# Scores of batches 3 and 4 formed transposed inside runs of small matmuls, with the runs at new steps, and loads of x released by ReLU results

## The chip, the cores and the metric

The kernel runs on one core of a Trainium2 chip. The metric is device time in microseconds (us) of one execution; smaller is better. Engines are named as in the profile: PE is TensorE (matmuls; PEld its weight loads), DVE is VectorE, ACT is ScalarE, POOL is GpSimd, and SP is SyncE, which here only issues transfers. A q behind an engine's name (SPq, POOLq) is its queue of issues.

## The reference: what is computed

There are 8 batches of 8 heads with 512 tokens each, 32 state rows per head, and 64 numbers per row; the feed-forward part has d_model 512 and d_ff 1536.

```
scores  = scale * x @ state^T            # per batch and head: 512 x 32
a       = softmax(scores)                # over the 32 state rows
xread   = a @ state                      # 512 tokens read from the state
scores2 = scale * state @ x^T            # 32 x 512
sread   = softmax(scores2) @ x           # 32 state rows read from the tokens
y       = concat([xread, sread])         # 544 rows per batch, 8 heads side by side = 512 numbers
out     = (relu(y @ w_gate) * (y @ w_val)) @ w_out
```

The output has 8 x 544 rows of 512 numbers in float32.

## The kernel before, in words

**Two products are merged.** Since `xread = a @ state`, the kernel forms `U = state @ w_gate` and `state @ w_val` once per batch (tile `U`, 256 rows of heads and states by 2 x 1536) and then `gate = a @ U`. The attention weights of a batch, transposed, are the tile `ans`.

**Step.** The main loop (line 547) runs over steps g = 12 b + jf from 28 to 107: batch b, slice jf of 128 of the 1536 columns. A step has a gate/value group (`gv`, line 319, or `gvs`, line 336, for the state rows at steps 96 to 107), four matmuls into two banks of PSUM; a ReLU of the gate on ACT (line 343, tile `g_sb`); the product with the value on DVE (line 347, tile `h_sb`); and a piece of the output product (`out_piece`, line 395), four matmuls on the `h_sb` of 18 steps ago (`lag`). Each third piece is followed by a copy on ACT (line 364) and an output transfer on SP. Then come the extra units of that step, in the order in which `at` was called for it.

**Extra units.** These prepare later batches:

- `x_load` (line 423): GpSimd issues the load of one batch of x, 512 KB after its cast to bf16, into one of four buffers `xb`.
- `x_trans_dma` (line 148): SP issues a transposing transfer from `xb` to `xT`.
- Scores, plain form (`att_sc`, line 173): eight matmuls of 64 columns for half the heads, with `xT` as weights. ACT takes the exponential to `e_sn` (line 203). A batch takes two such groups.
- Scores, transposed form (`sT_mm`, line 183): sixteen matmuls of 256 columns on 64x32 tiles of the array, eight side by side, with the state as weights, into two banks. ACT takes the exponential to `eT` (line 191), and a transposing transfer on SP turns it into `e_sn` (line 196).
- `att_norm`: for each half of the heads a sum and a reciprocal on DVE (lines 209, 211) and a scaling (line 215) on DVE or GpSimd; behind the second half, a transposing transfer on SP to `ans` (line 223).
- `u_unit` (line 292): eight matmuls of 512 columns on 64x32 tiles, a sixth of a batch's `U`; two casts out of PSUM on ACT and DVE (line 304).
- `x_pad` (line 251): two copies on GpSimd from `xb` to `xa`; `sr` (line 260): the state read `sread` of two batches, 128 matmuls of 65 columns on 128x32 tiles, normalised on DVE; `sr_T_dma` (line 274) transposes it through a transfer on SP, and `sr_out` copies it to `br` on ACT (line 278).
- `state_T_dma` (line 122) and `state_out_dma` (line 130): the state of batches 4 to 7, transposed by a transfer and copied by GpSimd.

**Runs.** `run` issues several units on small tiles one after another, because going from the whole array to small tiles and back costs time. A step with a run is in `paired`: it issues a second output piece behind the run, and the next step issues none. A run has two or three slots, a slot being a U unit or a transposed score. Before, batches 3 and 4 have plain scores, outside runs, at steps 28, 29, 39 and 40, and batches 5 to 7 transposed scores in the runs at 49, 61 and 73.

**Banks.** Eight banks of PSUM are named by tags. In the loop `bank` goes round three pairs, (4,3), (2,1), (0,5); a gate/value group takes one pair, a U unit or a transposed score too. Banks 6 and 7 hold output pieces and state reads. So in a run of three slots the third takes the pair of the gate/value group just before it, and waits for that group's ReLU and product.

**Order.** The kernel is scheduled by hand: each engine executes its instructions in the order in which the program issues them. Steps before 28 are a list of words (`program`, line 438), in which `gv.2.0@45` is the gate/value group of batch 2, slice 0, in banks 4 and 5, `re` and `mu` its ReLU and product, `dx` a load of x, `xd` a transposing transfer of x, `ad` one of attention, `xp` the pad copies. Each engine waits by semaphores for what it reads and for buffers to come free.

Of the kernel before, what the change touches and what calls it, by code (L numbers as in the profile page):

```python
# [9 lines left out]
BF16 = mybir.dt.bfloat16  # L10
# [6 lines left out]
def kernel(  # L17
# [9 lines left out]
    nc = tc.nc  # L27

    B, H, S, D = x.shape
# [34 lines left out]
    xa = const.tile([128, NX, NC * H, DP], BF16, name="xa")  # L64
# [4 lines left out]
    stT = const.tile([128, 2, B, H, Ns], BF16, name="stT")  # L69
# [2 lines left out]
    spare = hs_sb.rearrange("p f n -> p (f n)")  # L72
    warm = nc.const_aps.tensor(1.0, (128, 512), BF16)
    tiny = const.tile([128, 1], FP32, name="tiny")

    xf, xb, xT, eT, e_sn, a_sn, ANS, U, hsb = {}, {}, {}, {}, {}, {}, {}, {}, {}
    copy = {"act": nc.scalar.copy, "dve": nc.vector.tensor_copy, "pool": nc.gpsimd.tensor_copy}
# [14 lines left out]
    held = {}  # L92


    def state_dma(eng, lo, hi):
        src = state.rearrange("(g b) h (m i) d -> (b h m) g i d", b=2, i=4)
        eng.dma_start(out=st_f[:, lo // 2:hi // 2], in_=src[:, lo // 2:hi // 2])
# [64 lines left out]
    def sn_alloc(b):  # L162
        e_sn[b] = att.tile([128, 2, NC, NJ * Ns], BF16, name="e_sn", tag="e_sn", bufs=4)
        a_sn[b] = att.tile([128, 2, NC, NJ * Ns], BF16, name="a_sn", tag="a_sn")

    def att_sc(b, jp):
        if b not in e_sn:
            sn_alloc(b)
        t = held["sc", b, jp] = bank("sc_ps")
        ps = t.rearrange("p (r c j n) -> p r c j n", r=2, c=NC, j=2)  # L170
        for h in range(4 * jp, 4 * jp + 4):
            for k in range(2):
                nc.tensor.matmul(ps[:, h % 2, 2 * k:2 * k + 2, h // 2 % 2], xT[b][:, 2 * h + k], stT[:, :, b, h],  # L173
                                 start=True, stop=True)

    def sT_mm(b):

        held["sT", b] = [bank("sT_ps"), bank("sT_ps")]
        for parity in range(2):
            for j in range(NJ):  # L180
                h = 2 * j + parity
                for r in range(2):
                    nc.tensor.matmul(held["sT", b][r][32 * j:32 * j + 32, 256 * parity:256 * parity + 256],  # L183
                                     stT[64 * r:64 * r + 64, r, b, h],
                                     xT[b][64 * r:64 * r + 64, 2 * h:2 * h + 2].rearrange("p k t -> p (k t)"),
                                     start=True, stop=True)
# [232 lines left out]
    def x_load(b, part, parts):  # L419
        if part == 0:  # L420
            xb_alloc(b)
        hs = slice(H * part // parts, H * (part + 1) // parts)
        nc.gpsimd.dma_start(out=xb[b][:, hs], in_=x[b, hs].rearrange("h (p c) d -> p h c d", c=NC))  # L423
# [3 lines left out]
    def spin(n, cols=512):  # L427
        for i in range(n):
# [1 line left out]

    steps = {"spin": spin, "stc": state_conv, "stT": state_T, "sto": state_out, "xc": x_conv_pair, "xT": x_T, "on": lambda: nc.gpsimd.memset(xa[:, :, :, D:D + 1], 1.0), "dw": w_load, "dx": x_load, "ds": lambda: state_dma(nc.gpsimd, 2, B), "do": wo_dma,
             "xo": x_out, 
             "sc": att_sc, "ex": att_exp, "nr": att_sum, "nx": att_scale, "aT2": att_T2, "ao2": att_out2, "aT": att_T, "ao": att_out,
             "c": c_unit, "co": c_out, "u": u_unit, "uo": u_out, "gv": gv, "re": relu, "mu": mult, "o": out_part,
# [21 lines left out]
    gv.0.11@72 re.0.11 mu.0.11 mu.0.8 gv.1.9@63 gv.1.11@41 re.1.9 mu.1.9 gv.0.10@76 gv.1.6@20 re.1.11 re.0.10  # L458
    sc.2.1@4 gv.1.10@73 re.1.10 ex.2.1 re.1.6 mu.0.10 mu.0.9 o.0.3@6 sc.2.0@5 o.0.4 ex.2.0 o.0.0@7 mu.1.10 mu.1.11
    u.2.1.1024@43 mu.1.6 nr.2.1 uo.2.1.1024.1.act u.2.1.0@21 u.2.1.512@50 uo.2.1.512.1.act uo.2.1.1024.0.act  # L460
    uo.2.1.512.0.act uo.2.1.0.0.act nx.2.1 uo.2.1.0.1.dve o.0.1 o.0.5 stc.2.1.pool dx.3.0.1 xp.1 xp.0 xd.3 sr.1@3
    stc.3.0.pool nr.2.0 sr.0@0 nx.2.0 sn.1 u.2.0.0@14 ad.2 of.0.1.act u.2.0.1024@52 u.2.0.512@63 o.0.2 of.0.0.act
    uo.2.0.0.0.act uo.2.0.512.1.act uo.2.0.512.0.dve o.0.6@6 o.0.7 o.0.9@7 o.0.8 of.0.2.act sn.0 gv.1.8@01
    uo.2.0.0.1.dve uo.2.0.1024.0.dve gv.2.0@45 re.2.0 re.1.8 mu.1.8 gv.2.2@36 xp.3 gv.2.3@40 re.2.2 re.2.3 xp.2
    gv.2.1@31 re.2.1 mu.2.1 mu.2.3 mu.2.0 uo.2.0.1024.1.act mu.2.2
    """
    for word in program.split():
        word, _, banks = word.partition("@")
# [6 lines left out]
    units, paired = {}, set()  # L475

    def at(b, jf, f, *args):
        units.setdefault(NF * b + jf, []).append(lambda: f(*args))

    def att_up(b, kc, eng):  # L480
        att_sc(b, kc)
        att_exp(b, kc)
        att_norm(b, kc, eng)

    def att_norm(b, kc, eng):
        att_sum(b, kc)
        att_scale(b, kc, eng)
        if kc == 1:
            att_aT_dma(b)

    def run(*items):

        for it in items:
            if it[0] == "sT":
                sT_mm(it[1])
                for r in range(2):
                    sT_exp(it[1], r)
                eT_dma(it[1])
            else:
                u_unit(*it)  # L500
                for kc, eng in enumerate(("act", "dve") if len(items[0]) == 3 else ("dve", "dve")):
                    u_out(*it, kc, eng)

    def u(b, *part):
        order = (0, 0), (1, 0), (0, 512), (1, 512), (0, 1024), (1, 1024)
        return [(b, *order[i]) for i in part]

    def sr(*bs):
        sr_mm(bs, "spare")
# [2 lines left out]
    first, lag = 2 * NF + 4, 18  # L512
    for g in (2, 3):
        at(2, 2 + g, state_T_dma, g)
    for half in range(2):
        at(2, 5, state_out_dma, 2, half, "pool")
        at(2, 11, state_out_dma, 3, half, "pool")
    at(2, 5, x_load, 4, 0, 1)
    at(2, 10, x_load, 5, 0, 1)
    at(3, 10, x_load, 6, 0, 1)  # L520
    at(4, 10, x_load, 7, 0, 1)
    for b, s, jf in ((4, 2, 9), (5, 3, 6), (6, 4, 4), (7, 5, 4)):
        at(s, jf, x_trans_dma, b)
    for kc, eng in enumerate(("dve", "pool")):
        at(2, 4 + kc, att_up, 3, kc, eng)
        at(3, 3 + kc, att_up, 4, kc, "dve")
        at(4, 5 + kc, att_norm, 5, kc, "dve")
        at(5, 6 + kc, att_norm, 6, kc, "dve")
        at(6, 5 + kc, att_norm, 7, kc, "dve")
    for s, jf, items in ((2, 7, u(3, 0, 1, 2)), (2, 10, u(3, 3, 4, 5)),  # L530
                         (3, 7, u(4, 0, 1, 2)), (3, 10, u(4, 3, 4, 5)),
                         (4, 1, [("sT", 5)] + u(5, 0, 1)), (4, 10, u(5, 2, 3, 4)),
                         (5, 1, [("sT", 6)] + u(5, 5) + u(6, 0)), (5, 4, u(6, 1, 2, 3)), (5, 10, u(6, 4, 5) + u(7, 0)),
                         (6, 1, [("sT", 7)] + u(7, 1, 2)), (6, 10, u(7, 3, 4, 5))):
        at(s, jf, run, *items)
        paired.add(NF * s + jf)
    for bs, s, jf in (((2, 3), 2, 10), ((4, 5), 5, 4), ((6, 7), 6, 10)):
        at(s, jf, sr, *bs)
        at(s, jf + 1, sr_T_dma, bs)
        at(s, jf + 6, sr_out, bs, "act")  # L540
    for b, jf in ((0, 4), (1, 5)):
        at(2, jf, sr_T_dma, (b,))
        at(2, jf + 5, sr_out, (b,), "act")
    for b, s, jf in ((4, 3, 0), (5, 3, 9), (6, 5, 9), (7, 6, 0)):
        at(s, jf, x_pad, b)
    piece = first - lag
    for g in range(first, NF * (B + 1)):
        b, jf = divmod(g, NF)
# [47 lines left out]
```

## Time and profile before

| | us |
|---|---|
| median of 3 timed runs (lowest to highest) | 220.52 (220.29 to 220.78) |
| the profiled execution's own time | 219.6 |
| its span, first to last instruction | 217.8 |
| busy: PE, DVE, ACT, POOL | 213.4, 131.5, 119.3, 42.8 |
| gate/value groups, 384 matmuls (line 319) | 93.4 busy |
| output pieces, 372 matmuls (line 356) | 94.3 busy |
| plain scores, 80 matmuls (line 173) | 4.1 busy |
| transposed scores, 48 matmuls (line 183) | 1.2 busy |
| casts of U: DVE x40, ACT x32 (line 304) | 25.2, 16.7 busy |
| transfers that transpose: x, attention, scores, median to landing | 4.5, 3.1, 3.1 |

The page gives, for one execution, the busy time of each engine, the chain of work that ended last (followed back from the last instruction), and groups of instructions by line. The chain in order of time names, piece by piece, what the end of the kernel waited for. The timeline lists instructions with start and duration. "To landing" is the time from the issue of a transfer to its completion. The granted TensorE clock is full in this execution.

### The profile page before, as it was taken

Reading aid. Unit: us, or ns where it says so; the run is one execution under the profiler, and the core shown is the slowest. Engines: PE = TensorE matmul, PEld = TensorE weight load, DVE = VectorE, ACT = ScalarE, POOL = GpSimd, SP = SyncE. Lnnn points to the kernel's source line nnn. Section 1 sums busy time; section 2 is a strip of 40 time slices with the busy share of each in tenths; the row PEclk is TensorE's granted clock in tenths of the full one; section 3 lists DMA queues with packets and bytes.
Section 4 is the critical chain, followed back from the end, with each engine's and each line's share of the span. In section 5 each row is a group of like instructions: output and inputs, shape, how many; then the busy total and the mean of one; then the engine's idle time right before and its main releaser. Section 6 shows DMA issues by size and latency. Waiting matters only on the chain.

```text
span 217.8 us, 4862 instructions
## 1 busy us (share of the span) xinstructions
PE 213.4 (98%) x1957; PEld 105.2 (48%) x1957; DVE 131.5 (60%) x228; ACT 119.3 (55%) x229; POOL 42.8 (20%) x60
## 2 busy tenths in 40 slices
PE   8899999999999999999999999999999999999995
PEld 3554454454444454444444444444454445666544
DVE  5699977961986477657856778576765334222100
ACT  4698877746673666555445654764454543333222
POOL 7974049072154600000000070000000000000000
PEclk9999999999999999999999999999999999999999
DMA  7999999882879799317351651322411122222132
GB/s 166 182 195 198 199 224 164 118 207 81 120 116 156 153 201 178 89 51 158 84 101 48 132 124 21 98 62 63 102 50 60 48 48 50 51 51 85 61 96 97
DMA packets 45287, 24.44 MB, mean 112 GB/s; under 512 B 25712, under 2 KB 40944, under 8 KB 45264
## 3 DMA queue, kind: packets, MB, share of 16 engines
q0 software_dynamic: 16896, 9.05, 31.0%
q1 hardware_dynamic: 27472, 14.33, 27.6%
q10 hardware_dynamic: 896, 0.75, 1.3%
q8 instruction: 15, 0.25, 0.5%
q14 instruction: 8, 0.07, 0.1%
HBM read 18.35 MB, written 8.91 MB: 125 GB/s over the span
## 4 chain that ended last, share of the span: by engine, by line
PE 93%; DMA 3%; DVE 2%; issue 1%; POOL 0%; POOLq 0%
PE o_ps L356 40%; PE gv_ps L319 38%; PE gv_ps L336 5%; PE up L292 4%; DMA xb<-in_x_dram 3%; PE upc L292 1%; PE o_ps L385 1%; PE sr_ps L260 1%; PE xT_ps L156 1%; PE sc_ps L173 1%; DVE a_sn L215 1%; DVE cs L209 1%; PE sT_ps L183 0%; DVE xT L159 0%; DVE rc L211 0%
## 5 line engine op out<-in xcount | busy, mean ns | idle before, releaser
L356 PE MATMUL o_ps<-wo_sb,h_sb 128*128 128x512 bf16 x372 | 94.3, 379 | 0.0
L319 PE MATMUL gv_ps<-ans,U 128*128 128x512 bf16 x384 | 93.4, 379 | 0.0
L347 DVE TENSOR_TENSOR h_sb<-gv_ps,g_sb 128x512 bf16<-128x512 f32 x96 | 64.2, 687 | 46.6 <-ACT g_sb L343 45.7
L343 ACT ACTIVATE g_sb<-gv_ps 128x512 bf16<-128x512 f32 (+1 forms) x108 | 61.4, 579 | 47.2 <-PE gv_ps L319 35.0
L319 PEld LDWEIGHTS <-U 128*128 128x128 bf16 x384 | 36.8, 98 | 43.6 <-issue 0.8
L356 PEld LDWEIGHTS <-h_sb 128*128 128x128 bf16 x372 | 35.3, 98 | 41.8 <-issue 3.6
L364 ACT COPY o_sb<-o_ps 128x512 f32<-128x512 f32 x31 | 18.6, 598 | 18.6 <-PE o_ps L356 16.5
L251 POOL COPY xa<-xb 128x1024 bf16<-128x1024 bf16 x16 | 16.0, 1042 | 63.3 <-PE sr_ps L260 58.4
L304 DVE CAST U<-up 128x512 bf16<-128x512 f32 x40 | 25.2, 683 | 5.1 <-PE up L292 5.1
L304 ACT CAST U<-up 128x512 bf16<-128x512 f32 x32 | 16.7, 596 | 10.0 <-PE up L292 10.0
L347 DVE TENSOR_TENSOR hs_sb<-gv_ps,g_sb 128x256 bf16<-128x256 f32 x12 | 5.1, 425 | 15.3 <-PE gv_ps L336 10.5
L209 DVE TENSOR_REDUCE cs<-e_sn 128x16 f32<-128x512 bf16 x16 | 10.8, 677 | 2.0 <-ACT e_sn L203 2.0
L215 DVE TENSOR_TENSOR a_sn<-e_sn,rc 128x512 bf16<-128x512 bf16 x15 | 10.2, 686 | 0.4
L292 PEld LDWEIGHTS <-stT 64*32 64x32 bf16 x560 | 6.6, 91 | 7.1 <-issue 5.8
L314 ACT CAST U<-upc 128x512 bf16<-128x512 f32 (+1 forms) x19 | 8.7, 523 | 1.9 <-PE upc L292 1.9
L203 ACT ACTIVATE e_sn<-sc_ps 128x512 bf16<-128x512 f32 x10 | 6.0, 597 | 3.3 <-PE sc_ps L173 3.3
L429 PE MATMUL warm_ps<-const-bfloat16-1.0 128*128 128x512 bf16 (+2 forms) x17 | 6.8, 494 | 0.8 <-PEq L580 0.8
L336 PE MATMUL gv_ps<-br,wg_sb 128*128 128x256 bf16 x48 | 7.2, 273 | 0.0
L336 PE MATMUL gv_ps<-br,wv_sb 128*128 128x256 bf16 x48 | 7.2, 273 | 0.0
L423 POOL DMA_DIRECT2D xb<-in_x_dram x8 | 6.8, 857 | 0.6 <-DMA wg_sb<-in_moe_w_gate_dram 0.6
L292 PE MATMUL up<-wv_sb,stT 64*32 64x512 bf16 (+1 forms) x168 | 6.9, 348 | 0.0
L292 PE MATMUL up<-wg_sb,stT 64*32 64x512 bf16 (+1 forms) x168 | 6.9, 348 | 0.0
(57 smaller groups left out, 113.7 us busy)
## 6 DMA issues: line engine op xcount, KB each, us to landing
out_dram<-o_sb SPq DMA_DIRECT2D x26, 256.0 KB, 2.6
xb<-in_x_dram POOLq DMA_DIRECT2D x6, 512.0 KB, 8.2
wo_sb<-in_moe_w_out_dram POOLq DMA_DIRECT2D x2, 768.0 KB, 10.8
out_dram<-o_sb SPq DMA_DIRECT2D x11, 128.0 KB, 2.4
wg_sb<-in_moe_w_gate_dram POOLq DMA_DIRECT2D x5, 256.0 KB, 8.8
wv_sb<-in_moe_w_val_dram POOLq DMA_DIRECT2D x5, 256.0 KB, 9.5
xb<-in_x_dram POOLq DMA_DIRECT2D x3, 256.0 KB, 5.6
st_f<-in_state_dram POOLq DMA_DIRECT2D x1, 384.0 KB, 11.9
```

Of the source, the lines that this page charges most:

```text
L209: nc.vector.reduce_sum(out=cs, in_=e_v, axis=AX.X)
L215: {"dve": nc.vector, "pool": nc.gpsimd}[eng].tensor_tensor(out=by_pair(a_sn[b], jp).rearrange("p r (j n) -> p r j n", n=Ns), in0=e_v, in1= ...
L251: nc.gpsimd.tensor_copy(out=v[:, hs], in_=xb[b][:, hs])
L292: nc.tensor.matmul(dst[parity][32 * j:32 * j + 32], stT[r:r + 64, parity, b, 2 * j + parity], wsb[r:r + 64, j, lo:lo + n], start=True, sto ...
L304: copy[eng](out=U[b][:, w, kc, lo:lo + 512], in_=held["u", b, w, lo][kc])
L314: copy[eng](out=U[b][:, :, kc, lo:lo + n], in_=held["c", b, lo][kc])
L319: nc.tensor.matmul(ps[w], U[b][:, w, kc, f0:f0 + 128], ANS[b][:, kc].rearrange("p c t -> p (c t)"), start=(kc == 0), stop=(kc == NK - 1))
L336: nc.tensor.matmul(ps[w][:, 0:nt], wsb[:, j, f0:f0 + 128], br[:, j].rearrange("p b n -> p (b n)"), start=(j == 0), stop=(j == NJ - 1))
L343: nc.scalar.activation(out=g_sb[:, 0:n], in_=ps[0][:, 0:n], func=AF.Relu)
L347: nc.vector.tensor_tensor(out=dst, in0=ps[1][:, 0:n], in1=held["g", b, jf][:, 0:n], op=ALU.mult)
L356: nc.tensor.matmul(held["o", b, tsub], src[:, jf, tsub * 128:(tsub + 1) * 128], wo_sb[:, jf], start=(jf == 0), stop=(jf == NF - 1))
L364: copy[eng](out=o_sb, in_=held["o", b, tsub])
```

## The change

1. Batches 3 and 4 get transposed scores, as batches 5 to 7 have. The plain form in the loop and its helper `att_up` go; the one GpSimd scaling (batch 3, second half) goes to DVE.
2. The eleven runs become twelve, at new steps. U units are spread anew: five runs hold a score and two U units, six hold three U units, the last holds two. In runs with a score both casts of a U unit are on DVE, as before; in others one is on ACT and one on DVE. Scales stand three and four steps behind each score.
3. State reads move from steps 34, 64 and 82 to 34, 58 and 79, the pad copies and transposes of x with them.
4. `x_load_behind` copies one column of a ReLU's result `g_sb` to a new tile `mark` on GpSimd, and then issues the load of x. GpSimd works in order, so the load is not issued before that ReLU is done. Batches 4 to 7 are loaded in this way behind the ReLUs of steps 24 (in the word list), 34, 43 and 55; before, the loads stood at steps 29, 34, 46 and 58, behind nothing but what GpSimd had to do ahead of them.
5. In the word list, batch 3's transposing transfer of x moves behind batch 2's of attention, the ReLU and product of `gv.1.8` move ahead of those of `gv.2.0`, and each product follows its ReLU.

```diff
+    mark = const.tile([128, 1], BF16, name="mark")
...
+    def x_load_behind(b, gb, gj):
+
+        nc.gpsimd.tensor_copy(out=mark, in_=held["g", gb, gj][:, 0:1])
+        x_load(b, 0, 1)
...
-    uo.2.1.512.0.act uo.2.1.0.0.act nx.2.1 uo.2.1.0.1.dve o.0.1 o.0.5 stc.2.1.pool dx.3.0.1 xp.1 xp.0 xd.3 sr.1@3
-    stc.3.0.pool nr.2.0 sr.0@0 nx.2.0 sn.1 u.2.0.0@14 ad.2 of.0.1.act u.2.0.1024@52 u.2.0.512@63 o.0.2 of.0.0.act
+    uo.2.1.512.0.act uo.2.1.0.0.act nx.2.1 uo.2.1.0.1.dve o.0.1 o.0.5 stc.2.1.pool dx.3.0.1 xp.1 xp.0 sr.1@3
+    stc.3.0.pool nr.2.0 sr.0@0 nx.2.0 sn.1 u.2.0.0@14 ad.2 xd.3 of.0.1.act u.2.0.1024@52 u.2.0.512@63 o.0.2 of.0.0.act
...
-    uo.2.0.0.1.dve uo.2.0.1024.0.dve gv.2.0@45 re.2.0 re.1.8 mu.1.8 gv.2.2@36 xp.3 gv.2.3@40 re.2.2 re.2.3 xp.2
-    gv.2.1@31 re.2.1 mu.2.1 mu.2.3 mu.2.0 uo.2.0.1024.1.act mu.2.2
+    uo.2.0.0.1.dve uo.2.0.1024.0.dve gv.2.0@45 re.1.8 mu.1.8 re.2.0 mu.2.0 dxb.4.2.0 gv.2.2@36 xp.3 gv.2.3@40 re.2.2 mu.2.2 re.2.3 mu.2.3 xp.2
+    gv.2.1@31 re.2.1 mu.2.1 uo.2.0.1024.1.act
...
-    def att_up(b, kc, eng):
-        att_sc(b, kc)
-        att_exp(b, kc)
-        att_norm(b, kc, eng)
...
+        items = list(items)
+        scored = type(items[0]) is str
+        if scored:
+            b = int(items.pop(0)[2])
+            sT_mm(b)
+            for r in range(2):
+                sT_exp(b, r)
+            eT_dma(b)
+        while items:
+            b, i = items.pop(0), items.pop(0)
+            u_unit(b, *order[i])
+            u_out(b, *order[i], 0, "dve" if scored else "act")
+            u_out(b, *order[i], 1, "dve")
...
+    for b, g in ((5, 34), (6, 43), (7, 55)):
+        at(0, g, x_load_behind, b, *divmod(g, NF))
...
-    at(2, 5, x_load, 4, 0, 1)
-    at(2, 10, x_load, 5, 0, 1)
-    at(3, 10, x_load, 6, 0, 1)
-    at(4, 10, x_load, 7, 0, 1)
-    for b, s, jf in ((4, 2, 9), (5, 3, 6), (6, 4, 4), (7, 5, 4)):
-        at(s, jf, x_trans_dma, b)
-    for kc, eng in enumerate(("dve", "pool")):
-        at(2, 4 + kc, att_up, 3, kc, eng)
-        at(3, 3 + kc, att_up, 4, kc, "dve")
-        at(4, 5 + kc, att_norm, 5, kc, "dve")
-        at(5, 6 + kc, att_norm, 6, kc, "dve")
-        at(6, 5 + kc, att_norm, 7, kc, "dve")
-    for s, jf, items in ((2, 7, u(3, 0, 1, 2)), (2, 10, u(3, 3, 4, 5)),
-                         (3, 7, u(4, 0, 1, 2)), (3, 10, u(4, 3, 4, 5)),
-                         (4, 1, [("sT", 5)] + u(5, 0, 1)), (4, 10, u(5, 2, 3, 4)),
-                         (5, 1, [("sT", 6)] + u(5, 5) + u(6, 0)), (5, 4, u(6, 1, 2, 3)), (5, 10, u(6, 4, 5) + u(7, 0)),
-                         (6, 1, [("sT", 7)] + u(7, 1, 2)), (6, 10, u(7, 3, 4, 5))):
...
-    for bs, s, jf in (((2, 3), 2, 10), ((4, 5), 5, 4), ((6, 7), 6, 10)):
...
+    for b, g in ((4, 30), (5, 39), (6, 51), (7, 63)):
+        at(0, g, x_trans_dma, b)
+    for g, *items in ((28, "sT3", 3, 0, 3, 1), (34, 3, 2, 3, 3, 3, 4), (37, "sT4", 3, 5, 4, 0), (43, 4, 1, 4, 2, 4, 3),
+                      (49, "sT5", 4, 4, 4, 5), (55, 5, 0, 5, 1, 5, 2), (58, 5, 3, 5, 4, 5, 5), (61, "sT6", 6, 0, 6, 1),
+                      (67, 6, 2, 6, 3, 6, 4), (73, "sT7", 6, 5, 7, 0), (79, 7, 1, 7, 2, 7, 3), (85, 7, 4, 7, 5)):
+        at(0, g, run, *items)
+        paired.add(g)
+        if type(items[0]) is str:
+            for kc in range(2):
+                at(0, g + 3 + kc, att_norm, int(items[0][2]), kc, "dve")
+    for bs, g in (((2, 3), 34), ((4, 5), 58), ((6, 7), 79)):
+        at(0, g, sr, *bs)
+        at(0, g + 1, sr_T_dma, bs)
+        at(0, g + 6, sr_out, bs, "act")
...
-    for b, s, jf in ((4, 3, 0), (5, 3, 9), (6, 5, 9), (7, 6, 0)):
-        at(s, jf, x_pad, b)
+    for b, g in ((4, 36), (5, 42), (6, 60), (7, 66)):
+        at(0, g, x_pad, b)
```

More of the change, by code (lines that the diff above doesn't have):

```diff
@@ L429, in spin @@
             nc.tensor.matmul(warm_ps[:, 0:cols], warm[:, 0:128], warm[:, 0:cols], start=True, stop=True)
-    steps = {"spin": spin, "stc": state_conv, "stT": state_T, "sto": state_out, "xc": x_conv_pair, "xT": x_T, "on": lambda: nc.gpsimd.memset(xa[:, :, :, D:D + 1], 1.0), "dw": w_load, "dx": x_load, "ds": lambda: state_dma(nc.gpsimd, 2, B), "do": wo_dma,
+    def x_load_behind(b, gb, gj):
+        nc.gpsimd.tensor_copy(out=mark, in_=held["g", gb, gj][:, 0:1])
+        x_load(b, 0, 1)
+    steps = {"dxb": x_load_behind, "spin": spin, "stc": state_conv, "stT": state_T, "sto": state_out, "xc": x_conv_pair, "xT": x_T, "on": lambda: nc.gpsimd.memset(xa[:, :, :, D:D + 1], 1.0), "dw": w_load, "dx": x_load, "ds": lambda: state_dma(nc.gpsimd, 2, B), "do": wo_dma,
              "xo": x_out,
@@ L489, in att_norm @@
             att_aT_dma(b)
+    order = (0, 0), (1, 0), (0, 512), (1, 512), (0, 1024), (1, 1024)
     def run(*items):
[L493 to L506, printed above, removed]
+        items = list(items)
[11 more added lines that the diff above has]
+            u_out(b, *order[i], 1, "dve")
     def sr(*bs):
@@ L517 @@
         at(2, 11, state_out_dma, 3, half, "pool")
-    at(2, 5, x_load, 4, 0, 1)
-    at(2, 10, x_load, 5, 0, 1)
-    at(3, 10, x_load, 6, 0, 1)
-    at(4, 10, x_load, 7, 0, 1)
-    for b, s, jf in ((4, 2, 9), (5, 3, 6), (6, 4, 4), (7, 5, 4)):
-        at(s, jf, x_trans_dma, b)
-    for kc, eng in enumerate(("dve", "pool")):
-        at(2, 4 + kc, att_up, 3, kc, eng)
-        at(3, 3 + kc, att_up, 4, kc, "dve")
-        at(4, 5 + kc, att_norm, 5, kc, "dve")
-        at(5, 6 + kc, att_norm, 6, kc, "dve")
-        at(6, 5 + kc, att_norm, 7, kc, "dve")
-    for s, jf, items in ((2, 7, u(3, 0, 1, 2)), (2, 10, u(3, 3, 4, 5)),
-                         (3, 7, u(4, 0, 1, 2)), (3, 10, u(4, 3, 4, 5)),
-                         (4, 1, [("sT", 5)] + u(5, 0, 1)), (4, 10, u(5, 2, 3, 4)),
-                         (5, 1, [("sT", 6)] + u(5, 5) + u(6, 0)), (5, 4, u(6, 1, 2, 3)), (5, 10, u(6, 4, 5) + u(7, 0)),
-                         (6, 1, [("sT", 7)] + u(7, 1, 2)), (6, 10, u(7, 3, 4, 5))):
-        at(s, jf, run, *items)
-        paired.add(NF * s + jf)
-    for bs, s, jf in (((2, 3), 2, 10), ((4, 5), 5, 4), ((6, 7), 6, 10)):
-        at(s, jf, sr, *bs)
-        at(s, jf + 1, sr_T_dma, bs)
-        at(s, jf + 6, sr_out, bs, "act")
+    for b, g in ((4, 30), (5, 39), (6, 51), (7, 63)):
[12 more added lines that the diff above has]
+        at(0, g + 6, sr_out, bs, "act")
     for b, jf in ((0, 4), (1, 5)):
```

## The prediction

> **What bounds the kernel now.** I read the page's busy shares first, then its chain of work, then the chain in order of time through the main loop, then single rows.
>
> ```profile
> PE 213.4 (98%) x1957; PEld 105.2 (48%) x1957; DVE 131.5 (60%) x228; ACT 119.3 (55%) x229; POOL 42.8 (20%) x60
> ...
> PE 93%; DMA 3%; DVE 2%; issue 1%; POOL 0%; POOLq 0%
> ```
>
> TensorE is busy for 98% of the span and carries 93% of the chain. The other 7% stand before 13.3 us. From 49.5 us on every piece of the chain is a matmul, and each begins where the last ends. So in the loop a change of TensorE's own work moves the end one for one, work of any other engine moves it only by making TensorE wait, and there is no wait left to take away.
>
> The two ways of forming scores stand side by side in the chain (start, duration, piece):
>
> ```profile
> 54.71 0.86 PE o_ps L356 x4
> 55.58 0.23 PE sc_ps L173 x8
> 55.81 0.86 PE gv_ps L319 x4
> ...
> 61.22 0.77 PE up L292 x24
> 61.99 0.97 PE o_ps L356 x4
> ```
>
> ```profile
> 96.08 0.86 PE o_ps L356 x4
> 96.94 0.34 PE sT_ps L183 x16
> 97.28 0.43 PE up L292 x16
> 97.71 0.97 PE o_ps L356 x4
> ```
>
> A gate/value group and a quarter-output piece are 0.865 each (216 ns a matmul). The plain score group sc_ps adds 0.235 between them. A run costs 0.77 plus 0.10 on the piece behind it, 0.87, for three slots: three U units (61.22), or one transposed score and two U units (96.94). Two slots take 0.43, so a slot is 0.215, and 0.87 - 3 x 0.215 = 0.22 is what going into a run and out of it costs.
>
> **The change, part by part.** Times are of the profiled execution: span 217.8, its own time 219.6, so 1.8 around the span. The median of the runs shown is 220.52, 0.92 above it; I carry differences over to that median.
>
> *Scores on TensorE.* Batches 3 and 4 lose four plain groups: 4 x 0.235 = 0.94 less. They gain two transposed ones. Eleven runs hold 33 slots before (30 U units, 3 scores); after, twelve hold 35, eleven of three slots and the last, at step 85, of two. So exactly one run of two slots is added. No such run stands in the trace: bounds are its slots alone, 0.43, and a run of three, 0.87. I take 0.22 + 0.43 = 0.65. The three state reads stand in runs before and after, at 0.66 each. Sum on TensorE: -0.94 + 0.65 = **-0.29**, between -0.51 and -0.07.
>
> *Casts and scales.* U units beside a score are cast by VectorE alone: ten of them now, six before, so four casts (0.62 apiece in the 97.56 row) go from ScalarE to VectorE, and the scale that GpSimd did for batch 3 (1.05) becomes VectorE's (0.69). VectorE gets 3.2 on 131.5. What hides it is its idle time in the loop. This is how a pair of scales goes by there now (start, duration):
>
> ```profile
> 130.45 0.68 DVE L209 TENSOR_REDUCE cs<-e_sn 128x16 f32<-128x512 bf16 x1
> ...
> 132.06 0.68 DVE L347 TENSOR_TENSOR h_sb<-gv_ps,g_sb 128x512 bf16<-128x512 f32 x1
> 132.66 0.68 DVE L209 TENSOR_REDUCE cs<-e_sn 128x16 f32<-128x512 bf16 x1
> ...
> 134.37 1.23 SPq L223 DMA_TRANSPOSE ans<-a_sn  x1
> ```
>
> Sum, reciprocal and scale hold it 1.61, the product 0.60. A product normally starts 1.10 after its group (101.27 in the chain, 102.37 on VectorE). Scales now stand three and four steps behind a scored run, and two further steps on comes the next run. Counting from step g+3: product 1.10, scales 1.70, product 3.31, scales 3.91, product 5.52, product 6.29 (its normal time, 3 x 1.73 + 1.10). VectorE has caught up, by 0.1 to 0.2, when the run begins. A run's third slot takes the banks of that last product; in the run at 112.73 the product ends at 113.42 and the slot starts at 113.73, so 0.3 more is spare. Cost zero; with the cover gone, one for one.
>
> The Trainium skill (TensorEngine Tiling (Array Packing), PSUM Bottleneck) says that tiled matmuls speed up TensorE but not the evacuation of PSUM, and that the copies may then bound. By that, the saving is lost to VectorE's casts; the rows just counted leave 0.3 to 0.5 per run against it, and it is the second rival.
>
> *Program around step 28.* ReLU and product of the last batch-1 step go first, and each product directly behind its ReLU. VectorE waited 4.52 us there at 51.98, so products come earlier; nothing on the path. The first scored run starts at 55.58; its banks are free by then (a ReLU of 2.1 ends at 54.05, the last cast of U at 54.53). Batch 3's transpose of x moves behind batch 2's of attention on SP's queue: 44.2 + 1.2, then 4.6 to land, 50, against 55.58. Zero.
>
> *Loads held back.* Four copies of one column on GpSimd: not in the trace; between 0.10 (its memset of 128x1) and 1.04 (its 128x1024 copy), I take 0.10 as nearest. GpSimd is 20% busy. Behind the first copy wait the load of batch 4, four pad copies (4.0) and the state copies; their reader is the state read at step 34, ten microseconds on. Zero. The later copies hold nothing that is due within five.
>
> *The chain of batch 3.* Here cover is thin, so I follow it. Step 28's group stands at 53.85 in both kernels. After: piece to 55.58, run to 56.45, piece to 57.31, two groups to 59.04, piece to 59.91 = step 31; 32 at 61.64, 34 at 65.10, then 0.87 + 0.87 + run 0.87 + state read 0.66 + piece 0.87 puts step 35 at 69.23 and step 36, the first that needs batch 3's transposed attention, at 70.09. The score transpose is issued 1.56 behind the run's start (96.94 to 98.50): 57.14, and lands 3.1 later, 60.2; it is needed at 59.91 + 1.70 = 61.6. The load of batch 4, free at about 51.6 behind its ReLU, lands 6.0 later, 57.6, before the transpose moves much. SP's queue behind it holds two state-read transposes (1.2 each), one of the state (1.2), an output (0.3) and batch 4's transpose of x (2.2 to 2.6): 57.1 + 1.2 + 6.5 = 64.8, and another output to 65.2. By the count above, attention's transpose is issued at 59.91 + 3.91 + 1.71 = 65.5; at 3.1 it lands at 68.6, 1.5 early. But the load of batch 5 is let go by step 34's ReLU, at 65.10 + 1.10 = 66.2, only 0.8 behind it. What a load does to a transpose shows at 61.5:
>
> ```profile
> 61.42 0.94 POOL L423 DMA_DIRECT2D xb<-in_x_dram  x1
> 61.50 1.24 SPq L223 DMA_TRANSPOSE ans<-a_sn  x1
> ```
>
> ```profile
> L223 SPq DMA_TRANSPOSE ans<-a_sn x1: 1239/1239/1239, 61.5 to 61.5; - x1
> ...
> DMA to landing us min/median/max: 7.3/7.3/7.3
> ```
>
> ```profile
> L223 SPq DMA_TRANSPOSE ans<-a_sn x4: 1232/1238/1243, 82.3 to 155.2; - x4
> ...
> DMA to landing us min/median/max: 3.0/3.1/3.8
> ```
>
> Issued 0.08 behind a load it took 7.3 us, and clear of loads 3.0 to 3.8. The new order is transpose first. Bounds on its landing are 3.0 and 7.3; I take 3.1 to 3.8, since before the load's issue there is nothing it could wait for. Stall zero, at most 65.5 + 7.3 - 70.1 = 2.7.
>
> The Trainium skill (DMA: Bandwidth & Descriptors, Queues, rings and completion order) has each DMA engine take turns between queues packet by packet, and a completion mark land only after every earlier write of that engine, across queues. The 7.3 agrees; by that rule a load that starts while the transpose still moves can hold back its mark, which is the first rival.
>
> For batches 4 to 7 the scales come at 40, 52, 64 and 76 and attention is due at 48, 60, 72 and 84, over ten microseconds later; the loads at 43 and 55 are over before the next scores. The work behind step 107 is unchanged.
>
> Sum: -0.29. Profiled time 219.3; on the median **220.2**. About 0.2% (0.44 us) is what a measurement of this kernel can tell from no change, so the likeliest size lies under that.
>
> **Rivals.**
> 1. *Batch 3's attention comes late* (slower). Place: step 36. TensorE stalls by the landing time less 4.6 us. It decides from 4.9 us on, where the saving is gone, and passes 0.2% slower at 5.3. Midway between 3.1 and 7.3, at 5.2, the time is 220.8; at 7.3 it is 222.9. For it: 7.3, and a 6.7 for a transpose at 73.2 issued 0.7 behind a load. Against: the transpose leads by 0.8, and in before the same operand, 68.8 against 70.5, came in time even so.
> 2. *VectorE is late for the third slot* of runs 34, 43, 55, 67 and 79. At 0.1 to 0.2 each, 0.5 to 1.0: 220.7 to 221.2. For: 3.2 us more on it, scales nearer to the runs. Against: the count above.
> 3. *The timed runs hold stalls that the profile does not.* They are 0.92 longer. Before, two loads together (72.5 and 73.4) and four transposes of 6.7 to 9.0 us stand between 61 and 84; if the 0.92 is waiting there, spreading the loads gives it back: 220.52 - 0.29 - 0.92 = 219.3. Against: the profiled chain has no gap there.
> That holding the loads back does nothing is inside the forecast, which gives it nothing.
>
> **How the numbers follow.** Forecast 0.50, first rival 0.22, second 0.12, third 0.16. Of the forecast's half, a scatter of some 0.1% puts 0.18 on the fast side of 0.2% and 0.31 within. The first rival gives 0.16 to slower, 0.06 to within; the second 0.06 to each; the third 0.16 to faster, and 0.01 is over for slower. Faster 0.34, same 0.43, slower 0.23. The range is 219.4 to 221.5: below it stand some of the third rival, above it landings over 5.9 us.
>
> **What would show it.** Right: four sc_ps pieces gone from the chain; runs of 0.87 at steps 28 and 37; the run at 85 at 0.65; no gap between 49 and 204; ScalarE's 2.6 us wait on br at 71.8 gone without effect. Wrong: a TensorE gap before step 36 with attention's transpose over 4.6 us; gaps inside runs ending with a VectorE product; or gaps nowhere and still a change beyond 0.5 us, which would be the start or the third rival.

## The result, and the profile after

| | before | after |
|---|---|---|
| median of 22 timed runs each (lowest to highest), us | 220.34 (219.01 to 221.74) | 221.25 (220.55 to 222.40) |
| ratio to before, 95% interval | | 1.0036 (1.0021 to 1.0052) |
| the profiled execution's own time, us | 219.6 | 220.89 |
| its span, us | 217.8 | 219.1 |

The changed kernel is slower, by 0.36%. The time is inside the range of the prediction, and on the other side of no change than its forecast. Two pieces are missing from the forecast: TensorE waits 1.08 us once, at step 36, and the end of the kernel takes 0.37 us longer.

The first view is the page of after: its busy shares, and the shares of the chain of work that ended last.

```profile
PE 209.7 (96%) x1931; PEld 103.7 (47%) x1957; DVE 135.2 (62%) x233; ACT 118.1 (54%) x225; POOL 42.6 (19%) x63
...
PE 90%; DMA 5%; issue 2%; POOL 1%; ACT 0%; DVE 0%; POOLq 0%
```

TensorE's share falls from 98% to 96%, and from 93% to 90% of the chain. (1931 of its 1957 matmuls were recorded, so 213.4 and 209.7 are not to be subtracted. The starts of matmuls are what I compare.) A transfer now carries part of the chain. Which one, the chain of after in order of time shows (start, duration, piece):

```profile
54.83 0.86 PE o_ps L357 x4
55.69 0.34 PE sT_ps L184 x16
56.03 0.43 PE up L293 x16
...
65.20 0.45 PE gv_ps L320 x2
65.65 0.02 issue
65.67 0.45 ACT g_sb L344
66.12 4.94 DMA ans<-a_sn
71.06 0.05 issue
71.11 1.04 PE gv_ps L320 x4
```

Up to 65.20 it is the chain that was forecast: the plain scores are gone, and the run of step 28 stands at 55.69, of the forecast length. Then the chain leaves TensorE. The gate/value group at 71.11, step 36, was released by batch 3's attention transpose, issued at 66.12 and landed 4.94 later. (The 0.45 of ReLU ahead of it is where the profile puts what held that issue; the queue below shows what did.) The waits of after, in 55 to 75 us, name the same transfer (total, times, longest):

```profile
PEld L320 <- DMA ans<-a_sn: 1.4, 1, 1.4
...
PE gv_ps L320 <- DMA ans<-a_sn: 0.9, 1, 0.9
```

Matmuls of 0.216 start at 69.82 and at 71.11: 1.29 apart, a gap of 1.08. There is no other gap between 49 and 204. SP's queue in after, from the timeline (start, duration of the issue):

```profile
61.73 1.23 SPq L275 DMA_TRANSPOSE hs_sb<-sn  x1
63.05 1.94 SPq L149 DMA_TRANSPOSE xT<-xb  x1
65.08 0.95 SPq L369 DMA_DIRECT2D out_dram<-o_sb  x1
66.12 1.30 SPq L224 DMA_TRANSPOSE ans<-a_sn  x1
```

The scaling that the transpose waits for ended at 65.62. SP was then still issuing the output of step 32, until 66.03. So the transpose starts 0.5 late, and takes 4.94 where 3.1 to 3.8 was forecast. To be in time it had to land by 69.98.

The whole difference of the spans, by the starts of matmuls in the two traces:

| stretch, us | before | after | difference |
|---|---|---|---|
| start to the first matmul into `up` (line 293 of after) | 41.00 | 41.12 | +0.12 |
| from there to the last of the state rows' group (`gvs`), step 107 | 162.52 | 163.34 | +0.82 |
| from there to the last matmul | 11.39 | 11.39 | 0.00 |
| from there to the end of the span | 2.90 | 3.26 | +0.37 |

The +0.12 is scatter: that start stood anywhere from 40.6 (e10) to 42.7 (e4) in the profiles of this study. The +0.82 is the gap of 1.08, less 0.27 of TensorE's work.

### The profile page after: what moved, and what is told of

It reads as the page before. It is cut to its first block, busy times and chain, and to the rows that moved or that the text cites. A ratio compares the mean times of both kernels' runs of the same rounds, so it can differ in the third digit from the quotient of the medians.

```text
span 219.1 us, 4845 instructions
## 1 busy us (share of the span) xinstructions
PE 209.7 (96%) x1931; PEld 103.7 (47%) x1957; DVE 135.2 (62%) x233; ACT 118.1 (54%) x225; POOL 42.6 (19%) x63
## 4 chain that ended last, share of the span: by engine, by line
PE 90%; DMA 5%; issue 2%; POOL 1%; ACT 0%; DVE 0%; POOLq 0%
PE o_ps L357 38%; PE gv_ps L320 37%; PE gv_ps L337 5%; PE up L293 4%; DMA wv_sb<-in_moe_w_val_dram 3%; DMA ans<-a_sn 2%; PE upc L293 2%; PE o_ps L386 1%; PE sr_ps L261 1%; PE sT_ps L184 1%; POOL xb L424 1%; PE sc_ps L174 0%; PE aT_ps L232 0%; PE xT_ps L157 0%; POOL wg_sb L104 0%
## 5 line engine op out<-in xcount | busy, mean ns | idle before, releaser
L357 PE MATMUL o_ps<-wo_sb,h_sb 128*128 128x512 bf16 x354 | 90.6, 379 | 2.4 <-issue 2.2
L348 DVE TENSOR_TENSOR h_sb<-gv_ps,g_sb 128x512 bf16<-128x512 f32 x96 | 65.0, 688 | 43.8 <-ACT g_sb L344 42.6
L305 DVE CAST U<-up 128x512 bf16<-128x512 f32 x44 | 27.7, 683 | 5.8 <-PE up L293 5.8
L305 ACT CAST U<-up 128x512 bf16<-128x512 f32 x28 | 14.7, 595 | 9.0 <-PE up L293 9.0
L216 DVE TENSOR_TENSOR a_sn<-e_sn,rc 128x512 bf16<-128x512 bf16 x16 | 10.9, 686 | 0.5
L436 POOL COPY mark<-g_sb 128x1 bf16<-128x1 bf16 x4 | 0.8, 192 | 50.2 <-ACT g_sb L344 50.2
L192 ACT ACTIVATE eT<-sT_ps 128x512 bf16<-128x512 f32 x10 | 5.4, 594 | 5.2 <-PE sT_ps L184 5.2
L389 DVE COPY o_sb<-o_ps 128x64 f32<-128x64 f32 x2 | 0.5, 225 | 10.6 <-PE o_ps L386 10.5
```

What stands on the lines that cost most here:

```text
L216: {"dve": nc.vector, "pool": nc.gpsimd}[eng].tensor_tensor(out=by_pair(a_sn[b], jp).rearrange("p r (j n) -> p r j n", n=Ns), in0=e_v, in1= ...
L348: nc.vector.tensor_tensor(out=dst, in0=ps[1][:, 0:n], in1=held["g", b, jf][:, 0:n], op=ALU.mult)
L357: nc.tensor.matmul(held["o", b, tsub], src[:, jf, tsub * 128:(tsub + 1) * 128], wo_sb[:, jf], start=(jf == 0), stop=(jf == NF - 1))
```

## The experiments

Each edit is of the changed kernel unless it says otherwise. "The stretch of the loop" is the second row of the table above.

### 1. The scales of batch 3 one step earlier (e1, and again as e8)

```diff
-                at(0, g + 3 + kc, att_norm, int(items[0][2]), kc, "dve")
+                at(0, g + (2 if g == 28 else 3) + kc, att_norm, int(items[0][2]), kc, "dve")
```

> The changed kernel with batch 3's two scalings one step earlier (steps 30 and 31), so that its attention transpose is issued at about 65.0 instead of 66.1, nearly 2 us ahead of the load of batch 5. If the whole loss is the wait at step 36, the gap of TensorE there (1.08 us in the changed kernel) goes, from the first U unit to the last state-row group the loop takes 162.2 (before 162.52, changed 163.34), and the time against the kernel before is 0.9987. If the loss lies elsewhere too, the loop is shorter than 163.34 by less than 1 us and the ratio stays above 1.001.

Median 219.80, ratio 0.9987 (0.9967 to 1.0007). SP's queue in it, and how long the transpose took to land:

```profile
62.98 1.96 SPq L149 DMA_TRANSPOSE xT<-xb  x1
65.03 1.69 SPq L224 DMA_TRANSPOSE ans<-a_sn  x1
66.81 3.42 SPq L369 DMA_DIRECT2D out_dram<-o_sb  x2
```

```profile
DMA to landing us min/median/max: 3.5/3.5/3.5
```

The transpose is ahead of the output, is issued at 65.03 and lands at 68.53. The gap is gone, and the stretch of the loop is 162.25: 1.09 under after, 0.27 under before. So the wait at step 36 is all that the loop lost, and the saving on TensorE is there in the forecast size.

The same kernel was run again beside another:

> The kernel of the first experiment again (batch 3's scalings at steps 30 and 31), to narrow its interval: ratio 0.9987 to the kernel before if the 0.29 us of TensorE's work is all that is left of the change, 1.000 or more if something else takes it back in timed runs.

Median 219.86, ratio 0.9987 (0.9960 to 1.0015), and again 162.25 with no gap.

### 2. The load of batch 5 ahead of the transpose, and far behind it (e2, e3)

```diff
-    for b, g in ((5, 34), (6, 43), (7, 55)):
+    for b, g in ((5, 33), (6, 43), (7, 55)):   # e2
+    for b, g in ((5, 38), (6, 43), (7, 55)):   # e3, with the transpose of x of batch 5 at step 42 for 39
```

> The changed kernel with the load of batch 5 let go one step earlier, behind the ReLU of step 33, so that it is issued about 1 us ahead of batch 3's attention transpose instead of 0.7 behind it. If the load holds the transpose up, the transpose takes 6.5 to 7.5 us (7.3 in the kernel before, behind a load by 0.08) and the gap before step 36 grows from 1.1 to 2.5 or 3.5 us. If the transpose is late because of what SP has in front of it, the gap stays near 1.1.

> The changed kernel with the load of batch 5 held until the ReLU of step 38 and batch 5's transpose of x moved from step 39 to 42, so that no load is near batch 3's attention transpose, and SP's order in front of that transpose is as in the changed kernel. If the load is the cause, the transpose issued at 66.1 lands in 3.0 to 3.5 us, the gap before step 36 goes, and the time against the kernel before is 0.9987 unless the load now meets batch 4's transposes (then a gap at step 48 takes its place). If SP's queue is the cause, the transpose still lands at 70.5 or later and a gap of 0.5 or more stays.

With the load ahead, issued at 65.73, the chain of e2 shows the transpose at its longest:

```profile
66.64 11.46 DMA ans<-a_sn
78.11 0.05 issue
78.15 1.89 PE gv_ps L320 x4
```

11.46 to land, a gap of 7.57, and 229.5 us in the one run: a load ahead of a transpose, with the output directly ahead of it as well, costs far more than the 2.5 to 3.5 I expected. (The mean granted clock was 0.985, so I read the gap and not the whole time. The trace has it at 0.5 from 74.44 to 81.27, around the end of the gap: matmuls there start 0.427 apart instead of 0.216, and the loop is 1.5 longer than the gap explains.) In e3 the load is 11.8 us behind the transpose. GpSimd's and SP's rows of e3:

```profile
77.69 0.19 POOL L436 COPY mark<-g_sb 128x1 bf16<-128x1 bf16 x1 [7.43 <-ACT g_sb L344]
77.92 0.88 POOL L424 DMA_DIRECT2D xb<-in_x_dram  x1
```

```profile
65.12 0.95 SPq L369 DMA_DIRECT2D out_dram<-o_sb  x1
66.16 1.29 SPq L224 DMA_TRANSPOSE ans<-a_sn  x1
```

And it changes nothing: 4.93 to land, a gap of 1.07, median 221.00, ratio 1.0036 (1.0019 to 1.0053), as after. In after the load is issued at 66.85 and has no part in the late landing. That refutes the cause which my first rival named.

### 3. Batch 4's transpose of x behind batch 3's attention (e4)

```diff
-    for b, g in ((4, 30), (5, 39), (6, 51), (7, 63)):
+    for b, g in ((4, 33), (5, 39), (6, 51), (7, 63)):
```

> The changed kernel with batch 4's transpose of x moved from step 30 to 33, behind batch 3's attention transpose on SP; the load of batch 5 stays behind the ReLU of step 34. If SP's queue is the cause, the attention transpose is issued when its scaling ends, 65.65, lands at 68.7 to 69.1, and the gap before step 36 goes. If the load is the cause by itself, the transpose's lead on it grows from 0.7 to 1.2 us only, and it lands at 70.2 to 71 with a gap of 0.2 to 1.

This kernel ran 1.6 us later from its start. SP was free, the output was issued 1.6 ahead of the transpose, and the transpose went out as its scaling ended (67.27) and landed in 3.46: no gap at step 36. The chain of e4 shows the price paid elsewhere:

```profile
68.44 9.02 DMA xb<-in_x_dram
...
77.58 1.05 POOL xa L252
78.63 0.39 PE sT_ps L184 x16
```

The transpose of x, now beside the load of batch 5, took 4.27 to issue and 9.85 to land, and the scored run of step 37 waited 3.54. The one run took 226.53 (mean granted clock 0.992; here too it was 0.5 for 3.4 us, from 79.64). Emptying SP's queue by moving work into the load's time loses more than it wins. It does not say which of the two, the transpose of x or the output, made attention late.

### 4. Fewer warm-up matmuls, to move a packet of instructions (e5)

The trace records sixteen completion marks for a transfer, updates of its semaphore, and the transfer has landed with the last. For the transpose of after fifteen come at 69.35 to 69.51, the last at 71.06. One packet of 16,384 bytes of the queue that the page lists as

```profile
q8 instruction: 15, 0.25, 0.5%
```

ran from 69.06 to 70.01. The transpose ends with 32 packets of four bytes; thirty had started by 68.94, and the last two started as the packet of instructions ended (70.00 and 70.01). By this theory one DMA engine was busy with instructions, and the other fifteen were in time.

```diff
-    dw.1.256.256 dw.0.512.256 spin.8 stT.0@0 dw.1.512.256 ...
+    dw.1.256.256 dw.0.512.256 spin.1 stT.0@0 dw.1.512.256 ...
```

> The changed kernel with one warm-up matmul instead of eight at the start, that is 14 instructions of TensorE fewer ahead of the loop; its own start may come out later, and the loop alone is compared. In the changed kernel and with the load moved away, a 16 KB packet of the instruction queue occupies one DMA engine for 0.95 us from 69.03, just as the last packets of batch 3's attention transpose are due, and the last two of them start at 70.0. If that packet is what makes the transpose late, it now falls some 1.5 us later with respect to the loop, the transpose takes about 3.5 us instead of 4.9, and the gap before step 36 goes. If SP's queue alone is the cause, issue, landing and gap stay as they are, 4.9 us and 1.1.

One run, 220.96. The packet stayed (69.02), and so did the landing (4.94) and the gap (1.08). The edit did not move what it was to move: inconclusive. But the packet comes 2.5 to 3.0 us behind the issue of this transpose in after, e1, e3, e4, e5, e8 and two later kernels (e9, e10; in e2, beside the load, 7.7), wherever that issue stands, so it seems to go with SP's progress and not with TensorE's. Its presence alone does not decide, either: in e1 it ran from 67.89 and the marks came at 68.39 to 68.53.

The Trainium skill (DMA: Bandwidth & Descriptors, Why a DMA increments its semaphore by 16 and not by 1) says that the DMA engines of one transfer finish independently and that only the full count means that all has landed. The fifteen marks at 69.5 and the one at 71.06 agree with it. (Those of e5 stand the same way; in e3 all sixteen are recorded at 70.94 to 71.09.)

### 5. The hold alone, and the change without the hold (e6, e7)

e6 is the kernel before, with its loads of batches 4 to 7 held as in after (a word `dxb.4.2.0` behind `re.2.0`, then steps 34, 43, 55), and its scores and runs as they were. e7 is the changed kernel with plain loads at 29, 34, 46 and 58.

> The kernel before with the loads of batches 4 to 7 held behind the ReLUs of steps 24, 34, 43 and 55 as in the change, everything else as before. If holding the loads gives something by itself (waits of the timed runs that the profile of before does not show), it is up to 0.9 us faster, a ratio of 0.996. If before has nothing waiting for its transposes, its attention transpose of batch 3 lands in 3.1 us instead of 7.3 and the time stays within 0.2%: ratio 1.000.

> The changed kernel with the four loads put back to steps 29, 34, 46 and 58 without the copies, so that GpSimd issues them as soon as it gets there. If the hold is what makes early transposed scores possible, batch 4's and 5's loads now run back to back from about 55 to 70, the transposes of batch 3 take 7 to 11 us, and TensorE loses 3 to 10 us before step 36. If the loads do not matter as long as the transposes are short, the gap stays near 1.1.

e6: median 220.22 against 220.71, ratio 0.9984 (0.9961 to 1.0006). The interval holds no change, so a gain from holding alone is not shown; it would be under 0.9 us. In its profile the loop is even 0.40 longer (162.92), with a gap of 0.39 behind an attention transpose that took 7.45 from 108.64. e7: 227.57 in one run (granted clock 0.992), with some 6 us of gaps in and behind the first runs. The chain of e7 gives the cause:

```profile
57.26 9.34 DMA e_sn<-eT
66.60 0.02 issue
66.63 0.70 DVE cs L210
```

Loads issued at 56.34 and 57.21 stand beside batch 3's score transpose (issued at 57.26), which takes 9.34 instead of the 3.05 of after; VectorE is late from there on, and the runs wait for it. So holding is no saving in itself. It is what lets scores transposed by SP stand so early.

### 6. The output behind the transpose, and SP's queue emptied earlier (e9, e10)

```diff
+    late, LATE = [], (1, 0)                                        # e9: the output of step 32
...
-            nc.sync.dma_start(out=out_rows(b, tsub)[rows], in_=o_sb[rows])
+            send = lambda rows=rows: nc.sync.dma_start(out=out_rows(b, tsub)[rows], in_=o_sb[rows])
+            late.append(send) if (b, tsub) == LATE else send()
...
+        while late:                                                # behind the units of the step
+            late.pop()()
```

```diff
-    for g in (2, 3):
-        at(2, 2 + g, state_T_dma, g)
+    for g, jf in ((2, 28), (3, 40)):                               # e10: 29 becomes 40
+        at(0, jf, state_T_dma, g)
...
-        at(2, 11, state_out_dma, 3, half, "pool")
+        at(0, 45, state_out_dma, 3, half, "pool")
```

> The changed kernel, except that the output transfer of step 32 (out_dram, issued at 65.08 for 0.95 us, directly ahead of batch 3's attention transpose) is issued behind that transpose. Batch 4's transpose of x stays directly ahead, until 64.99. Theory A, the output ahead is what makes the transpose late (0.5 us of issue, and a last mark that lands 1.6 behind the others): the transpose is issued when its scaling ends, at 65.6, lands 3.4 to 3.6 later, at 69.0 to 69.2, before the 70.0 at which step 36 needs it; the 1.08 us gap goes, and the time is that of the kernel with the scales one step earlier, some 219.8, a ratio of 0.996 to 0.9995. Theory B, the transpose is slow for what else is under way (batch 4's transpose of x, the 16 KB packet of instructions): it lands 4.9 behind 65.6, at 70.5, and 0.5 us of the gap stay: 220.5 to 220.8.

> The changed kernel, except that the transpose of the state of batches 6 and 7 (60.43, 1.24 us of SP) goes from step 29 to step 40, and its copies on GpSimd from step 35 to step 45. SP is then 1.3 us earlier behind 60.4: batch 4's transpose of x is issued at 61.7, done with its issue at 63.7, and the output of step 32 is issued as soon as its copy is done, some 64.2 to 65.1. Theory A (what stands directly ahead of the transpose on SP, the output above all): with the output over by 64.6, the transpose is issued at 65.6 and lands 3.1 to 3.5 later, at 68.7 to 69.1; no gap before step 36, some 219.8, a ratio of 0.996 to 0.9995. If the output's copy ends only at 65.0, the output still stands directly ahead, the transpose is issued at 65.6 and by theory A still lands some 4.5 to 4.9 later, with a gap of 0.2 to 0.5. Theory B (the packet of instructions, which came 2.9 behind the transpose's issue in every run so far): 4.9 to land wherever the output is, 70.5, a gap of 0.5, and 220.5 to 220.8.

SP's queue in e9, with batch 4's transpose of x directly ahead as in after, and the landing of batch 3's attention:

```profile
63.01 1.94 SPq L149 DMA_TRANSPOSE xT<-xb  x1
65.61 1.26 SPq L224 DMA_TRANSPOSE ans<-a_sn  x1
66.97 3.30 SPq L371 DMA_DIRECT2D out_dram<-o_sb  x2
```

```profile
DMA to landing us min/median/max: 3.1/3.1/3.1
```

And SP's queue in e10, where the issue of the output ends 1.06 us before that of the transpose begins:

```profile
61.11 2.04 SPq L149 DMA_TRANSPOSE xT<-xb  x1
63.62 0.47 SPq L369 DMA_DIRECT2D out_dram<-o_sb  x1
65.15 1.25 SPq L224 DMA_TRANSPOSE ans<-a_sn  x1
```

It lands in 3.1 there too. Neither kernel has a gap, and the loop takes 162.25 in both. The packet of instructions ran in both as well, from 68.19 and 67.67, about 2.5 behind the issue. What decides in these kernels is the output issued directly ahead of the transpose, without a pause between them: it costs 0.5 of issue, and with it the landing takes 4.9 instead of 3.1 to 3.5 (4.94, 4.93 and 4.94 in after, e3 and e5, against 3.50, 3.54, 3.46, 3.11 and 3.06 in e1, e8, e4, e9 and e10). Of the two, the landing is what makes the stall: issued at 66.12 and landed 3.5 later, the transpose would have been in time for 69.98; issued at 65.62 and landed 4.94 later, it would still have been 0.6 late. How the output lengthens the landing stays open. A race with the packet of instructions fits: in after, e3 and e5 the last two four-byte packets of the transpose start as that packet ends or just behind, 0.9 to 1.1 after it began, and in e1, e8, e9 and e10 all of them have started by 0.15 after it began. But no run is without the packet, so this is not shown.

The times: e9 219.88, ratio 1.0001 (0.9985 to 1.0016); e10 219.65, ratio 0.9995 (0.9979 to 1.0011). I had expected 0.996 to 0.9995. With 0.27 less in the loop than before, e9 is level with before: something else costs.

### 7. The end of the kernel: two transfers fewer, and two more in the kernel before (e11, e12)

The last piece of the chain, which ends with the last copy out of PSUM, in before and in after:

```profile
215.14 0.22 DVE o_sb L388
```

```profile
216.08 0.23 DVE o_sb L389
```

From its end to the end of the span it is 2.45 in before (span 217.81) and 2.80 in after (219.11), though the last transfers are the same and land 1.98 behind the last matmul in both. The trace holds SP's final waits (the end of each, us; the last three of before, all eight of after):

```
before   216.44  216.61  | last landing 216.89 |  216.94
after    217.56          | last landing 217.83 |  217.88  217.94  218.00  218.06  218.12  218.18  218.24
```

The completion marks of SP's and ACT's transfers go round eight semaphores, and at the end SP waits for them one after another. Before issues 72 such transfers, nine on each semaphore, and the last to land is on the last in the order of waits. After issues 74, for it has two more transposes (of `eT`), and the last to land is on the second: six more waits of 0.061 follow, 0.37 us. Two kernels test that. e11 is e10 with two of five split outputs whole, so 72 transfers again; e12 is the kernel before with seven split outputs instead of five, so 74.

```diff
-        n = 2 if 4 * B - 9 <= 4 * b + tsub < 4 * B - 4 else 1
+        n = 2 if 4 * B - 7 <= 4 * b + tsub < 4 * B - 4 else 1      # e11
+        n = 2 if 4 * B - 11 <= 4 * b + tsub < 4 * B - 4 else 1     # e12
```

> The kernel of the preceding experiment (transpose of the state of batches 6 and 7 eleven steps later), except that two of the five outputs near the end of the loop that go as two transfers of 64 rows go as one of 128, so that the kernel issues as many transfers outside GpSimd as before (the two transposes of scores had added two). Theory, the tail: the completion marks of SP's and ACT's transfers go round eight semaphores, SP waits for the eight one after another at the end, some 0.06 us each, and two more transfers move the last landing from the last of these waits to the second, so that six waits follow it instead of none. Then the stretch from the last output matmul to the end goes from 3.28 us to 2.90, and nothing else changes: span 217.1 to 217.2 at the same start, some 0.37 us less than the preceding kernel, and against before 0.27 less: a ratio of 0.997 to 0.9995. Rival, the tail is longer for another reason (code, or the traffic of the last outputs): 3.28 stays, and so does the time of 219.65.

> The kernel before, except that seven outputs instead of five go as two transfers of 64 rows each, so that it issues two transfers more, as the changed kernel does; scores, runs and loads are those of before. Theory, the tail: the last landing moves to the second of the eight final waits, the stretch from the last output matmul to the end goes from 2.90 us to 3.26 to 3.29, and the time up by 0.37: a ratio of 1.0010 to 1.0025. Rival, the tail is longer for another reason: 2.90 stays and the ratio is 1.000.

The last piece of the chain in e11 (span 217.62), then in e12 (span 218.57):

```profile
214.93 0.23 DVE o_sb L389
```

```profile
215.54 0.23 DVE o_sb L388
```

2.46 and 2.80 to the end: the two have changed places. The last landing is on the last wait in e11, and on the second in e12, with six behind it. From the last matmul it is 2.92 in e11 (3.28 in e10) and 3.26 in e12 (2.90 before), with the loops as they were (162.25 and 162.52). Medians against before: e11 219.47, ratio 0.9973 (0.9950 to 0.9996); e12 220.93, ratio 1.0029 (0.9999 to 1.0058). The interval of e12 holds no change, so its 0.37 is shown by the profile and not by the time. The rival, a tail from the code or the traffic, is refuted by both profiles. e11 is faster than before, and by the ratios to before than after: it is the changed kernel with one transpose of state moved and two transfers fewer.

## Why the prediction was wrong

**The step that failed** is the one on batch 3's attention: "I take 3.1 to 3.8, since before the load's issue there is nothing it could wait for. Stall zero". It took 4.94, from an issue at 66.12 and not at 65.5, and the stall was 1.08. The bounds of 3.0 and 7.3 held; the choice near the lower one did not. The count had both causes in reach. It put "another output to 65.2" on SP's queue at 0.4, where the issue of an output took 0.53 at 59.81 and 0.95 at 65.08, and could only begin when that of batch 4's transpose of x was done. And it bounded the landing by the nearness of loads alone, while the runs show that an output directly ahead counts too (e9, e10).

**The first rival** had the place, the form of the price (landing less some 4.6, here less the 0.5 of late issue as well) and the sign: at 4.94 it gives a stall of 0.3 from an issue at 65.5, and 1.0 from the true one, against 1.08. Its cause was wrong. The load of batch 5 behind the transpose does nothing (e3); a load ahead would be ruinous (e2, 7.57). The rule that stood with it, of the Trainium skill (DMA: Bandwidth & Descriptors, Queues, rings and completion order), that DMA engines take turns between queues, agrees with the 11.46 of e2. That a load which starts behind the transpose holds back its mark is not what these runs show.

**A second term was missing.** "The work behind step 107 is unchanged" is true of the work, and the end still took 0.37 longer (e11, e12). I counted what each new transfer does on its queue and not that the kernel waits for every completion at its end. This term alone is larger than the forecast gain: without any stall, as in e9, the sum is -0.27 + 0.37, and the ratio of e9 is 1.0001. The times alone could not tell that sum (1.0005) from the -0.27 by itself (0.9988): the intervals of e1, e8, e9 and e10 hold both. The profiles tell, with 3.26 to 3.28 behind the last matmul in all four.

**What held.** TensorE's sum of -0.29 measured -0.27 in each kernel without the gap (162.25 against 162.52). The scored run of two U units at step 28 stood where forecast, and the score transpose was issued at 57.21 and landed at 60.26 (57.14 and 60.2). VectorE's 3.2 more were 3.7 (131.5 to 135.2), with 44 casts for 40 as counted, and no run's third slot waited: the second rival did not happen. The hold copies took 0.19 each (0.10 was taken) and hid behind GpSimd's idle time. ScalarE's wait on `br` went, without effect. The load of batch 4 was issued at 52.15 and landed at 57.96 (51.6 and 57.6).

**The third rival**, that timed runs hold waiting which holding the loads gives back, is not shown: e6 has 0.9984 with no change inside its interval. It is not excluded either, at up to 0.4%.

The sum of the profile is -0.27 + 1.08 + 0.37 = +1.18 on 219.6; the timed ratio gives +0.8 (0.46 to 1.15). The profiled executions are one of each kernel, so the last few tenths of this are not accounted for.

## What to carry to other kernels

When a step moves, follow the issuing queue itself to the transfer that is due, with each issue at the duration it will have in its new neighbourhood, and ask what stands directly ahead of it: here an issue 0.5 late and an output directly in front turned 1.3 us of slack (e9) into 1.08 of stall. Count the transfers of a change against those that the kernel waits for at its end as well. And when a saving is a few tenths, a rotation of semaphores can be worth more than it.

## What the runs showed of the hardware that I had not expected

- A transpose of 128 x 1024 through SP landed in 3.1 to 3.5 us with a transpose of x directly ahead, in 4.9 with an output directly ahead, and in 11.5 with that output and a 512 KB load issued 0.9 ahead.
- Two more transfers on SP made the end 0.37 us later, by six final waits of 0.061 that passed behind the last landing instead of ahead of it.
- Issues on SP stretch with what else moves: the transpose of x took 1.94 to issue behind the other transposes and 4.27 beside a load; an output 0.33 alone, 0.95 behind the transpose of x.
- A copy of one column on GpSimd took 0.19 us, and the load was issued 0.45 us behind the start of the copy (66.40 and 66.85).
- A long wait of TensorE cost more than itself: behind gaps of 7.57 (e2) and 3.54 (e4) matmuls started 0.427 apart instead of 0.216, at a granted clock of 0.5 that lasted 6.83 and 3.41 us, and the loops lost a further 1.5 and 1.6. Behind the 1.08 of after the clock stayed full.
